# A written order of all tasks in place of a list rule, with another weight split, other first loads and two units' taps on TensorE

## The chip, the cores and the metric

One core of one Trainium2 chip runs the whole program. The metric is the device time in microseconds of one execution, the median over several. A profiled execution gives a trace: TensorE (PE, and PEld for its weight loads), VectorE (DVE), ScalarE (ACT), GpSimd (POOL) and the DMA queue of SyncE (SP).

## The reference, cut to what matters

The program is a local attention with a few global rows, followed by a gated layer over all heads. There are 8 batches and 8 heads; each head has 512 local rows and 32 global rows of width 64. A global row attends to all 544 keys; a local row to the 32 global keys and to the local keys within 32 positions.

```python
s_g = scale * np.matmul(q_g, k_all.transpose(0, 1, 3, 2))
out_g = np.matmul(sm(s_g), v_all)
...
s_ll = np.where(np.abs(pos[:, None] - pos[None, :]) <= 32, s_ll, -1000000000.0)
s_l = np.concatenate([s_lg, s_ll], axis=-1)
out_l = np.matmul(sm(s_l), np.concatenate([v_g, v_l], axis=2))
x = np.concatenate([out_g, out_l], axis=2)          # then heads side by side: (8, 544, 512)
...
for k in range(5):
    gate_pre += conv_w[k] * xp[:, k:k + S, :]       # causal, along the sequence
gate = 1.0 / (1.0 + np.exp(-gate_pre))
return (gate * (x @ w_val) @ w_out).astype(np.float32)
```

The inputs are float32, the three parameters of the gated layer float64.

## The kernel before, in words

**Units.** A unit is two heads of one batch, 128 channels: 32 units, four to a batch. Every piece of work is a task with a name, and the number in a name is the unit, or the batch for the global rows.

- `iq`, `iv` load a unit's queries and keys (a `qk` tile, 624 KB) and its values (a `v` tile, 975 KB); `fq`, `fv` mark the buffers free. There are four buffers of each.
- `s` (L419): 64 small fp32 matmuls, scores of 16 blocks of 32 rows against 128 keys, for both heads, into PSUM tiles sx and sy.
- `mx` u.h (L431), VectorE: adds the mask and takes the row minimum of the negated scores, four fused operations a head. `exp` (L438), ScalarE. `t` (L444): four transposes on TensorE. `tc` (L447): ScalarE copies them to SBUF.
- `av` (L455): 64 matmuls with the values. `norm` (L462, L463, L465), VectorE, divides by the sums. `xt` (L474): four transposes back. `xc` (L478): a ScalarE copy.
- `halo` (L483, L485) puts the last global rows ahead of the unit. `xh` (L503, ScalarE) rounds to the fast matmul format fp32r, `xl` (L506, VectorE) is the rest. So products are made of three matmuls: high times high, high times low, low times high.
- The gate is five taps along the sequence: `tap` (L497) and `conv` u.0 to u.3 (L510), all on VectorE. In the first NPC = 3 units they are fp32 matmuls with diagonal matrices instead: `dg` (L524, ScalarE makes the diagonals), `pc` u.0 to u.4 (L535), copied out by ScalarE (L540). The first NHF = 1 unit does not wait for the global rows and is mended by `fix` (L492).
- Global rows of a batch: `gs` (L344), `gmax` (L351 to L353), `gexp` (L360, L361), `gt` (L367 to L370), `gtc` (L376 to L378), `gav` (L387), `gnorm` (L393 to L395), `gx` (L399), `gxc` (L403).

**Gated layer.** `sig` (L543) is the sigmoid. `g1.b.e.t` (L559) multiplies by w_val, three matmuls for each input tile t and output tile e; `gv` (L567, VectorE) times the gate, `gh` (L570, ScalarE) and `gl` (L573, VectorE) split it, `g2.b.r.e` (L581) multiplies by w_out, `ob` (L586, ScalarE) copies out, `st` stores. The global rows of all batches go through it last, as batch g: `gxh`, `gxl` (L624, L627), `gconv` (L630, L632: one scaling and four taps each), `sigg`, then g1.g and g2.g.

**Weights.** The eight 128-row tiles of w_val and w_out come as float64 bits in pairs of int32. Tasks `w`k.s0 to s5 (L245 to L252) on VectorE rebuild a float32 value and a low remainder, ScalarE rounds the value to fp32r (`w`k.high, L297), and VectorE subtracts the rounded from the value (`less`, L301) and adds the remainder (`plus`, L304) to make the low part.

**Order.** The kernel is written task by task into strict in-order queues, one for each engine. `Plan.order` (L140 to L207) makes the order by a list rule: from planned durations, delays and buffer rings it computes when each ready task could begin, and takes the earliest, ties by the priorities PR. Nothing of it runs on the chip.

```python
                    if best is None or (at, t.prio) < best[0]:
                        best = ((at, t.prio), t)
```

**Start.** `first` lists the loads that are issued before the plan. GpSimd zeroes a tile zf, VectorE casts it to zr, and `keep_clock` (L641) issues matmuls of zeros: WARM = 4 at the start, and more in planned gaps over KEEP = 1500 ns until the first task that takes an `mm` PSUM bank.

Of the kernel before, what the change touches and what calls it, by code (L numbers as in the profile page):

```python
# [19 lines left out]
KW = 5  # L20
# [24 lines left out]
def pos_chunk(p):  # L45
# [3 lines left out]
PR = {'w': (2.1108, 2.3658, 2.2497, 1.6373, 1.8399, 2.1059, 1.8007, 2.1913),  # L49
      'whigh': 2.271,  # L50
      'gs': 4.588,
      'gmax': 2.96,
      's': 1.721,
      'mx': 0.684,
      'exp': 2.812,
      'norm': 1.347,
      'xl': 5.608,
      'tap': 3.042,
      'conv': 3.339,
      'pc': 5.493,  # L60
      'gv': -3.126,
      'gl': 0.929,
      'wi': -1.844,
      'cw': -4.483,
      'dg': 3.265,
      'sig': 1.801,
      'ob': 0.619,
      'gh': -3.407,
      'tc': 0.686,
      'xc': -1.569,  # L70
      'xh': 1.612,
      't': 1.915,
      'av': 3.833,
      'xt': 3.243,
      'g': 6.355,
      'gexp': 5.157,
      'gt': 2.783,
      'gtc': 1.05,
      'gav': 0.635,
      'gnorm': 1.312,  # L80
      'gx': -0.882,
      'gxc': 3.072,
      'fix': 4.315}
E1 = D + 1
NX = 10
NHF = 1
NQ = 4
WO = 2
NPC = 3
WARM = 4  # L90
# [15 lines left out]
class Task:  # L106
    __slots__ = ("name", "eng", "cost", "deps", "take", "give", "prio", "emit", "end", "start", "lock")

    def __init__(self, name, eng, cost, deps, take, give, prio, emit, lock):
        self.name, self.eng, self.cost, self.deps = name, eng, cost, deps  # L110
        self.take, self.give, self.prio, self.emit, self.lock = take, give, prio, emit, lock
        self.start = self.end = None


class Plan:
# [13 lines left out]
    def add(self, name, eng, cost, emit, deps=(), take=(), give=(), prio=5.0, lock=False):  # L129
        assert name not in self.tasks, name  # L130
        self.tasks[name] = Task(name, eng, cost, tuple(deps), tuple(take), tuple(give), prio, emit, lock)
# [8 lines left out]
    def order(self):  # L140
        users, missing, todo = {}, {}, {}
        done = dict(self.ready)
        for t in self.tasks.values():
            todo.setdefault(t.eng, [])
            names = {d for d in t.deps if d not in done}
            missing[t.name] = len(names)
            for d in names:
                users.setdefault(d, []).append(t)
            if not names:
                todo[t.eng].append(t)  # L150
        free = dict.fromkeys(todo, 0.0)
        held = dict.fromkeys(LOCKED, 0.0)
        mode, table = 2, 1
        line, base = [], {}

        def since(t):
            at = base.get(t.name)
            if at is None:
                at = base[t.name] = max([0.0] + [done[d] + self.lag(d, t) for d in t.deps])
            more = {}  # L160
            for name, _ in t.take:
                n, taken, freed = self.rings[name]
                k = len(taken) + more.get(name, 0) - n
                more[name] = more.get(name, 0) + 1
                if k >= 0:
                    if k >= len(taken) or taken[k] not in freed:
                        return None
                    at = max(at, freed[taken[k]])
            return at

        while len(line) < len(self.tasks):
            best = None
            for eng, ts in todo.items():
                for t in ts:
                    at = since(t)
                    if at is None:
                        continue
                    if t.lock:
                        at = max(at, held[LOCKED[eng == "DVE"]])
                    at = max(at, free[eng])  # L180
                    if best is None or (at, t.prio) < best[0]:
                        best = ((at, t.prio), t)
            if best is None:
                raise RuntimeError("nothing can begin: " + ", ".join(t.name for ts in todo.values() for t in ts))
            (at, _), t = best
            for name, key in t.take:
                self.rings[name][1].append(key)
# [10 lines left out]
            for name, key in t.give:  # L198
                assert key in self.rings[name][1], (t.name, name, key)
                self.rings[name][2][key] = t.end + LAG[t.eng]  # L200
            todo[t.eng].remove(t)
            for user in users.get(t.name, ()):
                missing[user.name] -= 1
                if not missing[user.name]:
                    todo[user.eng].append(user)
            line.append(t)
        return line  # L207
# [3 lines left out]
def attention_moe(ctx, tc, qk, vw, maskd, w_val, convT, w_out, out):  # L211
# [21 lines left out]
    xgT = cp.tile([P, NDT, B, KW - 1 + SG], F32, name="xgT")  # L233
    zf = sb.tile([P, SL], F32, tag="gv", name="zf")
# [3 lines left out]
    def f64_parts(raw, a, e, b):  # L238
# [5 lines left out]
        af = a.bitcast(F32)  # L244
        return (lambda: V.tensor_scalar(out=a, in0=hi, scalar1=0x7FFFFFFF, scalar2=None, op0=ALU.bitwise_and),  # L245
# [9 lines left out]
    def taps():  # L255
        raw = craw.rearrange("p (n two) -> p n two", two=2)
        a = sb.tile([P, NDT * KW], I32, tag="mx", name="cva", bufs=3)
        for step in f64_parts(raw, a, raw[..., 1], raw[..., 0].bitcast(F32)):
            step()
# [604 lines left out]
```

## Time and profile before

| | |
|---|---|
| median of three runs | 380.77 us (380.75 to 383.97) |
| profiled execution, its own time | 384.15 us |
| its span, first to last instruction | 382.3 us |
| instructions | 14802 |
| busy: PE, PEld | 363.6 us (95%), 281.9 us (74%) |
| busy: DVE, ACT, POOL | 312.0 us (82%), 263.7 us (69%), 2.2 us (1%) |
| mean granted TensorE clock | 0.993 |
| DMA | 66.74 MB, mean 175 GB/s |

In the rows of the profile, `PE po L581` is an engine, the tile that it writes and the line of the kernel; `x48` is a count of instructions; `<-ACT pm L438 3.0` says what ended an idle time, and for how many us. Matmuls are pipelined, so their durations overlap; what one costs TensorE is the distance to the next one's start. The same holds, by a smaller overlap, for VectorE and ScalarE. A wait on "issue" is time in which the engine waited for nothing that the profile shows.

### The profile page before, as it was taken

The numbers are of one execution on the slowest core, as the hardware profiler recorded it, in microseconds if no ns is written. First come the engines' busy times: TensorE is split into PE (matmuls) and PEld (weight loads), VectorE is DVE, ScalarE is ACT, GpSimd is POOL, SyncE is SP. The second block draws the span as 40 slices with busy tenths as digits, with TensorE's granted clock in tenths as the row PEclk, the third lists the DMA queues.
The fourth block names the chain that finished last, engine by engine and source line by source line (L and its number), as shares of the span: only waits on it lengthen the run. The fifth ranks groups of instructions, "written<-read, shape, count | busy, mean of one in ns | idle before, by whom it ended". The sixth has DMA issues, their size and how long they took to land.

```text
span 382.3 us, 14802 instructions
## 1 busy us (share of the span) xinstructions
PE 363.6 (95%) x6342; PEld 281.9 (74%) x6342; DVE 312.0 (82%) x1089; ACT 263.7 (69%) x624; POOL 2.2 (1%) x8
## 2 busy tenths in 40 slices
PE   6797999999999999999899979999999999999994
PEld 4455567777777788877777768777877888888893
DVE  4997999999968997689878987699699999996230
ACT  2986379966899578966795669659996776413221
POOL 2000000000000000000000000000000000000000
PEclk9998999999999999999999999999999999999998
DMA  8996873846521973556382646564663011020112
GB/s 274 406 405 236 295 259 115 280 179 230 187 69 38 394 269 107 223 189 224 117 310 77 235 141 182 231 186 155 256 210 106 4 57 58 0 83 29 55 57 56
DMA packets 17250, 66.74 MB, mean 175 GB/s; under 512 B 1952, under 2 KB 4000, under 8 KB 17184
## 3 DMA queue, kind: packets, MB, share of 16 engines
q1 hardware_dynamic: 17184, 65.79, 48.1%
q8 instruction: 50, 0.82, 0.9%
q14 instruction: 16, 0.13, 0.1%
HBM read 56.87 MB, written 8.91 MB: 172 GB/s over the span
## 4 chain that ended last, share of the span: by engine, by line
PE 62%; DVE 22%; ACT 10%; DMA 2%; issue 2%; SPq 0%; ACTq 0%
PE po L581 21%; PE pv L559 14%; PE ax L455 6%; PE pt L444 5%; ACT pm L438 5%; DVE gate L510 4%; PE sx L419 3%; PE ax L474 3%; DVE pm L431 2%; DVE gl L573 2%; PE ag L387 2%; DVE xs L465 2%; PE sy L419 2%; PE pvg L559 1%; PE pog L581 1%
## 5 line engine op out<-in xcount | busy, mean ns | idle before, releaser
L438 ACT ACTIVATE pm<-pm,mx 128x128 f32<-128x128 f32 x256 | 80.8, 393 | 17.9 <-DVE mx L431 17.8
L510 DVE SCALAR_TENSOR_TENSOR gate<-xc,cw,gate 128x512 f32<-128x512 f32 x116 | 84.5, 747 | 0.5
L581 PE MATMUL po<-woh,gh 128*128 128x512 f32 x128 | 54.4, 425 | 0.0
L559 PE MATMUL pv<-xh,wvh 128*128 128x512 f32 x128 | 54.0, 422 | 0.0
L559 PE MATMUL pv<-xl,wvh 128*128 128x512 f32 x128 | 50.6, 396 | 0.0
L581 PE MATMUL po<-woh,gl 128*128 128x512 f32 x128 | 50.4, 394 | 0.1
L559 PE MATMUL pv<-xh,wvl 128*128 128x512 f32 x128 | 50.5, 394 | 0.0
L581 PE MATMUL po<-wol,gh 128*128 128x512 f32 x128 | 50.1, 392 | 0.0
L444 PE MATMUL pt<-ident,pm 128*128 128x128 f32 x256 | 41.4, 284 | 4.0 <-ACT pm L438 3.8
L447 ACT COPY pts<-pt 128x512 f32<-128x512 f32 x64 | 36.8, 584 | 9.5 <-PE pt L444 9.3
L444 PEld LDWEIGHTS pt<-ident,pm 128*128 128x128 f32 x256 | 30.6, 142 | 14.3 <-ACT pm L438 5.8
L419 PE MATMUL sx<-qk 64*32 64x128 f32 x1024 | 38.7, 278 | 0.0
L419 PE MATMUL sy<-qk 64*32 64x128 f32 x1024 | 37.3, 278 | 0.1
L455 PEld LDWEIGHTS ax<-v,pts 128*32 128x32 f32 x2048 | 30.9, 111 | 7.6 <-issue 3.6
L419 PEld LDWEIGHTS sx<-qk 64*32 64x32 f32 x1024 | 29.3, 107 | 9.8 <-issue 4.6
L455 PE MATMUL ax<-v,pts 128*32 128x65 f32 x2048 | 36.2, 223 | 0.3 <-ACT xc L478 0.3
L586 ACT COPY ob<-po 128x512 f32<-128x512 f32 x32 | 18.8, 588 | 21.9 <-PE po L581 21.7
L570 ACT CAST gh<-gv 128x512 fp32r<-128x512 f32 x32 | 19.7, 617 | 17.8 <-DVE gv L567 17.8
L567 DVE TENSOR_TENSOR gv<-pv,gate 128x512 f32<-128x512 f32 x32 | 22.0, 688 | 11.1 <-PE pv L559 9.4
L431 DVE CUSTOM_DVE_ANT_0 pm<-sx,mask 128x128 f32<-128x128 f32 x128 | 29.4, 286 | 1.7 <-PE sx L419 1.6
L573 DVE TENSOR_TENSOR gl<-gv,gh 128x512 fp32r<-128x512 f32 x32 | 22.0, 689 | 10.5 <-ACT gh L570 10.4
L431 DVE CUSTOM_DVE_ANT_0 pm<-sy,mask 128x128 f32<-128x128 f32 x128 | 29.4, 287 | 0.0
(109 smaller groups left out, 658.4 us busy)
## 6 DMA issues: line engine op xcount, KB each, us to landing
v<-in_vw_dram SPq DMA_DIRECT2D x32, 975.0 KB, 7.7
qk<-in_qk_dram SPq DMA_DIRECT2D x32, 624.0 KB, 5.0
out_dram<-ob SPq DMA_DIRECT2D x32, 256.0 KB, 2.3
wraw<-in_w_val_dram SPq DMA_DIRECT2D x4, 512.0 KB, 12.3
wraw<-in_w_out_dram SPq DMA_DIRECT2D x4, 512.0 KB, 8.0
out_dram<-obg SPq DMA_DIRECT2D x8, 64.0 KB, 1.7
mask<-in_mask_dram SPq DMA_DIRECT2D x1, 256.0 KB, 4.2
craw<-in_convT_dram SPq DMA_DIRECT2D x1, 20.0 KB, 3.9
```

The source lines that it names most:

```text
L419: T.matmul((sx, sy)[h][32 * j:32 * j + 32, i, :], qkt[rows, 32 * m:32 * m + 32], qkt[rows, k0:k0 + P], start=True, stop=True)
L431: V.tensor_tensor_reduce(out=pm[:, h, i, :], in0=s[:, i, :], in1=mask[:, i, :], op0=ALU.add, op1=ALU.min, scale=-SCALE, scalar=3.0e38, acc ...
L438: A.activation(out=pm[:, h, i, :], in_=pm[:, h, i, :], func=AF.Exp, bias=mx[:, c:c + 1], scale=-1.0)
L444: T.transpose(pt[:, i, :], pm[:, h, i, :], ident)
L447: A.copy(st[u]["pts"][:, h], st[u]["pt", h])
L455: T.matmul(ax[32 * j:32 * j + 32, h, E1 * i:E1 * i + E1], pts[:, h, i, 32 * j:32 * j + 32], vt[:, block_win(4 * i + j), h, :], start=True, ...
L510: V.scalar_tensor_tensor(out=acc, in0=xc[:, k:k + SL], scalar=cw[:, u % NDT, k:k + 1], in1=acc, op0=ALU.mult, op1=ALU.add)
L559: T.matmul(box["pv", e], w[:, e, t * P:t * P + P], x, start=(t == 0 and q == 0), stop=(t == NDT - 1 and q == 2))
L567: V.tensor_tensor(out=box["gv", e], in0=box["pv", e], in1=gates[x0 + e], op=ALU.mult)
L570: A.copy(box["gh"][:, e, :], box["gv", e])
L573: V.tensor_tensor(out=box["gl"][:, e, :], in0=box["gv", e], in1=box["gh"][:, e, :].bitcast(F32), op=ALU.subtract)
L581: T.matmul(box["po", r], g[:, e, rs], w[:, e, :], start=(e == 0 and q == 0), stop=(e == NDT - 1 and q == 2))
```

## The change

It does five things.

1. The list rule and its priorities go. `ORDER` is a text of 1494 task names; each engine gets its tasks in that order. `Plan.order` still computes planned times, for the filler matmuls alone.
2. The weights are split by bits: step s2 keeps 12 bits fewer, so that the value in `a` is already the high part. The low part is made of the bits left over by four more VectorE steps (s4 to s7 in place of s4, s5, less and plus). ScalarE's rounding copy `high` stays. (`PW` names no tile, so the branch with GpSimd is not taken; `NXP` = 0 likewise.)
3. First loads: q3 moves from behind v0 to ahead of it.
4. Start: zf is zeroed on VectorE, ScalarE runs one exponential on it, and warm-up is two fp32 matmuls of zf and one of zr (WARM 4 to 1). Of xgT only the halo columns are zeroed. Fillers for gaps become more numerous (0.55 for 0.4 of the gap).
5. NPC goes from 3 to 2, NHF from 1 to 2: units 0 and 1 have their taps on TensorE and are mended by `fix`. NTA = 4: `tap` of units 2 and 3 goes to ScalarE.

```diff
-PR = {'w': (2.1108, 2.3658, 2.2497, 1.6373, 1.8399, 2.1059, 1.8007, 2.1913),
...
+ORDER = """
+cw s0 mx0.0 exp0.0 mx0.1 w0.s0 exp0.1 first s1 mx1.0 exp1.0 w0.s1 t0.0 w0.s2 tc0.0 t1.0 tc1.0 t0.1 mx1.1 tc0.1 gs0
+w0.s3 w0.s4 w0.s5 w0.s6 gmax0.0 dg0 exp1.1 av0 gexp0.0 iq4 t1.1 gmax0.1 w1.s0 iq5 gexp0.1 s2 norm0 lq4 tc1.1 xt0 w1.s1
+w0.s7 w1.s2 w0.high mx2.0 mx2.1 xc0 exp2.0 halo0 gt0.0 w2.s0 w1.s3 av1 w2.s1 norm1 s3 w1.s4 pc0.0 w2.s2 dg1 w1.s5
...
+g1.2.3.3 sig11 conv15.3 gv.2.2 sig12 gl.2.1 gv.2.3 mx19.0 xt17 mx19.1 gt4.1 gh.2.2 lq20 g2.2.0.0 xl16 gl.2.2 xc17
+g2.2.0.1 iq23 av18 lq23 gtc4.1 gh.2.3 gav4.1 s20 g2.2.0.2 tap16 sig13 gnorm4.1 gx4 gl.2.3 mx20.0 exp19.1 g2.2.0.3 gxc4
...
+st.6.3 g1.7.3.0 gxl2 gv.7.2 gxh3 st.6.2 g1.7.3.1 g1.7.3.2 g1.7.3.3 gh.7.2 g2.7.0.0 g2.7.0.1 gl.7.2 g2.7.0.2 gv.7.3
+gh.7.3 gl.7.3 g2.7.0.3 gconv3 gxl0 g2.7.1.0 g2.7.1.1 g2.7.1.2 ob.7.0 gconv0 g2.7.1.3 g2.7.2.0 gconv1 g2.7.2.1 gconv2
+g2.7.2.2 st.7.0 ob.7.1 st.7.1 g2.7.2.3 g2.7.3.0 g2.7.3.1 g2.7.3.2 ob.7.2 g2.7.3.3 g1.g.0.0 g1.g.0.1 g1.g.0.2 ob.7.3
+gxl3 sigg g1.g.0.3 st.7.3 gv.g.0 st.7.2 g1.g.1.0 gh.g.0 g1.g.1.1 g1.g.1.2 g1.g.1.3 g1.g.2.0 g1.g.2.1 gl.g.0 g1.g.2.2
...
+"""
+PW = "x"
+NXP = 0
+FIRST = "q0 m0 q1 w0 q2 q3 v0 w1 v1 w2 v2 w3 v3"
+NTA = 4
-NHF = 1
+NHF = 2
-NPC = 3
-WARM = 4
+NPC = 2
+WARM = 1
...
-                    if best is None or (at, t.prio) < best[0]:
-                        best = ((at, t.prio), t)
...
+        for name in ORDER.split():
+            put(self.tasks[name])
...
+        kept = 0x3FFFFFF8 if low is None else 0x3FFFF000
...
+        power = lambda: V.tensor_scalar(out=hi, in0=a, scalar1=-0x00800000, scalar2=None, op0=ALU.bitwise_and)
+        scaled = lambda x, out: V.scalar_tensor_tensor(out=out, in0=x, scalar=2.0 ** -52, in1=hf, op0=ALU.mult,
+                                                       op1=ALU.mult)
...
+        return first + (lambda: V.tensor_scalar(out=hi, in0=hi, scalar1=0x1FF, scalar2=None, op0=ALU.bitwise_and),
+                        lambda: V.scalar_tensor_tensor(out=lf, in0=hi, scalar=2.0 ** 32, in1=lo.bitcast(U32),
+                                                       op0=ALU.mult, op1=ALU.add),
+                        power, lambda: scaled(lf, low))
...
-        plan.add(f"w{k}.less", "DVE", 570, less, [f"w{k}.high", f"w{k}.s5"], prio=prio - 0.01, lock=True)
-        plan.add(f"w{k}", "DVE", 570, plus, [f"w{k}.less"], give=back, prio=prio - 0.02, lock=True)
...
+        if u < NTA:
+            A.activation(out=g, in_=x, func=AF.Copy, scale=w)
+        else:
+            V.tensor_scalar(out=g, in0=x, scalar1=w, scalar2=None, op0=ALU.mult)
...
-        G.memset(zf, 0.0)
-        V.tensor_copy(zr, zf)
-        G.memset(xgT, 0.0)
+        G.memset(xgT[:, :, :, :KW - 1], 0.0)
+        A.activation(out=table, in_=zf[:, :1], func=AF.Exp)
+        keep_clock(2, zf)
         keep_clock(WARM)
...
-                    keep_clock(int((gap - 300) * 0.4 / 235))
+                    keep_clock(int((gap - 400) * 0.55 / 235))
```

378 lines of the change are left out of this document (198 added, 180 removed).

## The prediction, as it went on record

> **What bounds the kernel now.** I read the stage windows first, then the end of the chain of waits, then the groups of TensorE and VectorE on both sides of 182.5 us.
>
> The rows give length, then busy us (and instructions) of TensorE, its weight load, VectorE, ScalarE and GpSimd, the granted TensorE clock, DMA share and GB/s.
>
> ```profile
> 0.00:40.00 40.00, 31.25 (x641) 20.20 (x645) 31.36 (x128) 28.16 (x77) 2.16 (x8) 0.96 0.85 317
> 40.00:100.00 60.00, 59.33 (x1205) 42.99 (x1204) 59.13 (x214) 42.44 (x107) 0.00 (x0) 1.00 0.65 229
> 100.00:182.50 82.50, 82.50 (x1577) 65.25 (x1566) 68.66 (x258) 66.64 (x152) 0.00 (x0) 1.00 0.53 187
> 182.50:322.60 140.10, 135.96 (x2684) 108.12 (x2683) 121.53 (x435) 109.34 (x258) 0.00 (x0) 1.00 0.45 156
> 322.60:382.30 59.70, 54.54 (x262) 45.37 (x260) 31.29 (x62) 17.13 (x32) 0.00 (x0) 0.98 0.14 49
> ```
>
> The reader is to see three stages. Until 40 us nothing is full: loads at 317 GB/s, TensorE and VectorE waiting for each other. From 40 to 100 us TensorE (59.33 of 60) and VectorE (59.13) are both full. After 100 us TensorE alone is full and VectorE has slack (13.8 us idle of 82.5). ScalarE never binds for long. The end is pure TensorE:
>
> ```profile
> 355.10 10.91 PE po L581 x48
> 366.01 5.69 PE pvg L559 x48
> 371.70 5.46 PE pog L581 x24
> ```
>
> That is 0.227 us for a product matmul of 512 columns, 0.119 us for one of 256, and a last matmul that is over at 377.16, 5.1 us before the span ends. So the time is TensorE's work, plus what TensorE waits in the head and in a few later places, plus 5.1 us.
>
> **The change, part by part.** The forecast is made at one cut: the moment when the new list lets g2.2.0.3 start (third batch, second product, the one that waits for gl.2.3). Up to there VectorE's list is the longest demand; behind it TensorE's is.
>
> *Remaining work behind the cut.* These TensorE groups ran in the old kernel from 182.5 us to its last matmul:
>
> ```profile
> L581 PE MATMUL po<-woh,gh 128*128 128x512 f32 x83 | 34.8, 419 | 0.0
> L559 PE MATMUL pv<-xh,wvh 128*128 128x512 f32 x80 | 33.1, 413 | 0.0
> ...
> L455 PE MATMUL ax<-v,pts 128*32 128x65 f32 x960 | 16.7, 221 | 0.0
> L444 PE MATMUL pt<-ident,pm 128*128 128x128 f32 x112 | 16.7, 276 | 3.0 <-ACT pm L438 3.0
> L419 PE MATMUL sx<-qk 64*32 64x128 f32 x416 | 15.0, 273 | 0.0
> ...
> L474 PE MATMUL ax<-ident,xs 128*128 128x128 f32 x64 | 10.1, 278 | 1.0 <-issue 1.0
> ```
>
> In tasks: 83 second products of the batches (and 8 of the global stage), 80 first products, 15 av, 28 t, 13 s (416 of sx and as many of sy), 16 xt. Counted in the written list from g2.2.0.3 on: 93 and 8 second products, 80 first ones, 13 av, 26 t, 11 s, 14 xt. Ten second products more (30 matmuls of 0.227 = 6.8 us) against two av, two t, two s, two xt and three small tasks fewer. With the busy times of the rows (16.7/15 an av, 16.7/28 a t, 15.0/13 an s, 10.1/16 an xt) the four pairs are 7.0 us. So the work behind the cut equals that of the old kernel behind 182.5 us, which took 377.16 - 182.5 = 194.7 us, 4.0 of it waits (3.0 for an exponential, 1.0 called issue). (The busy times hold an overlap with the next task, which the three small tasks make up.)
>
> *When the cut comes, by VectorE.* Its work before 182.5 us in the old kernel:
>
> ```profile
> L510 DVE SCALAR_TENSOR_TENSOR gate<-xc,cw,gate 128x512 f32<-128x512 f32 x47 | 34.2, 747 | 0.2
> ...
> L431 DVE DVE_READ_ACCUMULATOR2_ANT mx<- 128x1 f32 x148 | 12.5, 84 | 0.0
> L465 DVE TENSOR_TENSOR xs<-ax,mx 128x512 f32<-128x512 f32 x17 | 11.8, 692 | 0.6
> L506 DVE TENSOR_TENSOR xl<-xc,xh 128x512 fp32r<-128x512 f32 x15 | 10.3, 688 | 0.6 <-ACT xh L503 0.5
> ...
> L395 DVE TENSOR_SCALAR xg<-ag,gd 128x64 f32<-128x64 f32 x9 | 2.6, 284 | 0.3
> ...
> L492 DVE SCALAR_TENSOR_TENSOR gate<-xgT,cw,gate 128x4 f32<-128x4 f32 (+3 forms) x4 | 0.9, 220 | 0.1
> ```
>
> An instruction's share of the engine is its distance to the next start, some 0.09 us under its duration:
>
> ```profile
> 20.43 0.71 DVE L249 SCALAR_TENSOR_TENSOR wa<-wraw,wa 128x512 int32<-128x512 int32 x1
> 21.04 0.70 DVE L506 TENSOR_TENSOR xl<-xc,xh 128x512 fp32r<-128x512 f32 x1
> 21.64 0.43 DVE L245 TENSOR_SCALAR wa<-wraw 128x512 int32<-128x512 int32 x1
> 21.98 0.45 DVE L251 TENSOR_SCALAR wraw<-wa 128x512 int32<-128x512 int32 x1
> ...
> 24.79 0.30 DVE L431 CUSTOM_DVE_ANT_0 pm<-sx,mask 128x128 f32<-128x128 f32 x1
> ...
> 25.00 0.30 DVE L431 CUSTOM_DVE_ANT_0 pm<-sx,mask 128x128 f32<-128x128 f32 x1
> ```
>
> So an operation with two tensors holds VectorE 0.60, one with a scalar 0.34, a tap (747 ns) 0.66, a masked maximum (four with their reads, each 0.21) 0.85.
>
> The written list has ahead of gl.2.3: 56 taps on VectorE against 47 (+5.9, four of them because unit 2 loses its TensorE taps), 40 half maxima against 148/4 = 37 (+2.5), 18 norms against 17 (+1.0), 17 xl against 15 (+1.2), one more norm of the global rows and one more set of four halo fixes (together +1.5). All eight weight tiles lie ahead in both. A tile was four short and four long operations (s0, s1, s2, s4; s3, s5, less, plus): 3.76 us; now five short and three long (less and plus give way to an AND and a multiply-add inside the raw words, then power and scale): 3.50, so -2.1 for eight. The new operations have no row; the nearest, L245 and L251 with a stride on one side and L249 with one on an input, give 0.34 and 0.60, and I take these; strided on both sides they could cost 0.60 instead of 0.34, at most +2.1 in all, and not less than nothing. Sum: +10.0.
>
> VectorE's old busy time up to 182.5 us is 31.36 + 59.13 + 68.66 = 159.2, of which 1.2 come before its real start:
>
> ```profile
> 1.80 1.24 DVE L788 CAST zr<-zf 128x512 fp32r<-128x512 f32 x1 [1.80 <-POOL zf L787]
> 5.61 0.18 DVE L245 TENSOR_SCALAR cva<-craw 128x20 int32<-128x20 int32 x1 [2.57 <-DMA craw<-in_convT_dram]
> ```
>
> The new kernel needs 158.0 + 10.0 = 168.0 us from 5.6 on. Idle to add, by VectorE's waits of the first 100 us:
>
> ```profile
> DVE mx L462 <- PE ax L455: 1.6, 1, 1.6
> DVE wa L245 <- DMA wraw<-in_w_val_dram: 0.8, 1, 0.8
> DVE wa L301 <- ACT wvh L297: 0.5, 1, 0.5
> DVE gd L393 <- PE ag L387: 0.4, 1, 0.4
> ```
>
> The third is gone, since the low part no longer waits for ScalarE's rounded copy; 2.8 stay. From 40 to 100 us VectorE lost 0.87 in 60; over the 138 us to the cut 2.0. Cut at 5.6 + 168.0 + 4.8 = 178.4 us.
>
> *The same by TensorE.* Five fp32 taps of unit 2 go. Sixteen instructions, two to a tap, show their price:
>
> ```profile
> 43.42 7.03 PE L535 MATMUL pc<-xc,diag 128*128 128x512 f32 x16
> ```
>
> 0.43 each, so 5 x 2 x 0.43 = 4.3 us. TensorE at the old pace would be at the cut at 182.5 - 4.3 = 178.2. The two engines agree within 0.2 us: the first half gains 4.1 us, and neither has room to spare.
>
> *Head.* ScalarE's first exponentials start late:
>
> ```profile
> 7.15 1.28 ACT L524 ACT_TABLE_LOAD   x1 [7.15 <-DVE cw L260]
> ...
> 9.92 2.44 ACT L438 ACTIVATE pm<-pm,mx 128x128 f32<-128x128 f32 x8
> ```
>
> The table load moves ahead of the data and the first diagonals behind the exponentials: up to 2.8 us for ScalarE, of which I count nothing, because VectorE's demand hides it; without that cover it would be a gain. v0 behind q3 costs av0 a qk tile's transfer and gives it to gs0, which the list puts ahead of av0: nothing. The two zero-filled fp32 warm-up matmuls (four instructions, 0.43 at full clock, 0.86 at half, so 1.7 to 3.4 us) run before the first scores have data, and cw is ahead of the first maximum anyway: nothing, at worst 0.3.
>
> *Behind the cut.* A written order can place an exponential earlier: the 3.0 us go (they could all return). The 1.0 called issue stays. Changes between kinds of TensorE task are 299 in the old timeline and 301 in the list: nothing. SP's queue is reordered too; I followed each load from the task that frees its buffer to its first user. Most have over 8 us; v14, v15, v23 and v24 have 5 to 7: nothing, at worst 1 us each. ScalarE gets two taps of 0.5 us and loses unit 2's diagonals and its copy: hidden.
>
> At the tail the list puts all four global taps behind gl.7.3, and gxl3 behind them:
>
> ```profile
> 335.07 0.35 DVE L630 TENSOR_SCALAR gateg<-xgT,cw 128x256 f32<-128x256 f32 x1
> 335.45 2.05 DVE L632 SCALAR_TENSOR_TENSOR gateg<-xgT,cw,gateg 128x256 f32<-128x256 f32 x4
> ```
>
> After the last g1.7 VectorE needs about 2.2 us for gv and gl with ScalarE's copy between, 4 x 2.43 for these taps, and two splits of 0.34: 12.6 us. TensorE has 10.91 us of second products and three parts of g1.g (9 x 0.119 = 1.1) before g1.g.0.3 wants gxl3: it waits 0.6 us, 0 to 1.
>
> Sum: 178.4 + 194.7 - 3.0 + 0.6 + 5.1 = 375.8 us against a span of 382.3, so -6.5. The profiled execution's own time was 384.15 us, 1.85 more than its span and 3.4 above the median of the runs, 380.77 (380.75 to 383.97); I take the difference off the median: **374.3 us**.
>
> **Rivals.**
>
> *TensorE was the only limit.* VectorE idles 2.0 instead of 4.8, no wait returns, the issue wait and the tail wait go: -2.8 - 1.6, 369.9 us. For it: the loads of the head leave ScalarE's 2.8 us on the table. Against it: the two sums above agree, so each engine's waits become the other's.
>
> *The gain turns into new waits.* The order is fixed for planned durations; where an instruction is late, all behind it on its engine wait. VectorE idles 8 us (+3.2), the 3.0 us for exponentials come back: 380.5 us. For it: VectorE's idle was 4.2 us in the head and up to 100 us (3.3 of the rows above and 0.87) even under a rule that was free to choose. Against: that rule planned blind too.
>
> *The clock.* Once in the old head, after 1.05 us of TensorE work in 3.0, the granted clock halved for a stretch (first fence), though the longest gap was under 2 us (second):
>
> ```profile
> 28.20:31.20 3.00, 1.05 (x51) 0.73 (x41) 2.65 (x18) 2.14 (x7) 0.00 (x0) 1.00 1.01 412
> 32.13:35.55 3.42, 3.18 (x50) 2.45 (x52) 2.38 (x6) 3.06 (x7) 0.00 (x0) 0.50 0.53 173
> ```
>
> ```profile
> 30.68 0.55 PE L387 MATMUL ag<-v,pgt 96*32 96x65 f32 x23 [1.95 <-issue]
> ```
>
> Such a stretch costs up to 1.7 us. Filler matmuls stop at the first pc0.0, fourteenth on TensorE's list, while VectorE's demand still grows 6.5 us faster than TensorE's work between s4 and g1.0.0.3, by the prices above. Two more stretches: +3.4, 377.7 us. The Trainium skill (TensorE: Matmul & The Clock Gate, "Why this matters for your kernels") says that gaps up to about 3 us between bursts are safe; by that rule these stretches cost nothing and the forecast stands. The trace is stricter, since 1.95 us was enough.
>
> *Slower.* From 100 us to the cut VectorE idled 13.8 us, harmlessly, since it was ahead. If the strict list makes it idle as much while it is the limit, waiting for scores or products that are listed late, its idle at the cut is 4.8 + 13.8 = 18.6 and the cut 13.8 us later: 388.1 us. It decides from 15.1 us of idle on (4.8 plus the 10.3 us between 374.3 and 1% above the old median). For it: the list has no second choice. Against: 40 to 100 us show 0.87 idle in 60 when VectorE has a backlog.
>
> *It does not do what it says.* The rounded high part is still ScalarE's copy; if the new bit operations cost the upper bound, +2.1, 376.4: inside the range.
>
> **How the numbers follow.** Forecast 0.57 (370.5 to 376.9), TensorE alone 0.10, new waits 0.15, clock 0.10, slower 0.08. A measurement here tells about 1% from no change, 377.0 to 384.6 being the same. Faster 0.57 + 0.10 = 0.67, same 0.15 + 0.10 = 0.25, slower 0.08. The range runs from just above the first rival, 370.0, to 381.0, half a microsecond above the new waits: left out are half the first rival and the slower case and a little of the waits.
>
> **What would show it.** In the new profile: 20 pc matmuls instead of 30; VectorE over 97% busy from 40 us to the cut, and the cut (the 36th second product's start) near 178 us; behind it TensorE without a wait over 1.5 us; g1.g waiting half a microsecond for xgl. I am wrong if VectorE idles over 8 us after 40 us with TensorE idle in the same places, or if the cut is in time and the second half has new waits, of loads above all.

## The result, and the profile after

The new kernel takes 400.18 us (median; 396.43 to 403.6) against 381.31 us for the old one on the same chip: ratio 1.042, 95% interval 1.037 to 1.048. The forecast was 374.3 us: the change is slower where I expected it faster, and the miss is 26 us. The profiled execution took 399.97 us with a span of 397.3.

The stage windows of the new kernel, in the same cuts and columns as in the prediction:

```profile
0.00:40.00 40.00, 29.86 (x647) 18.40 (x648) 30.68 (x142) 25.26 (x71) 0.85 (x7) 0.96 0.81 303
40.00:100.00 60.00, 53.73 (x1013) 39.00 (x1012) 54.36 (x186) 40.24 (x95) 0.00 (x0) 1.00 0.57 211
100.00:182.50 82.50, 77.67 (x1768) 61.21 (x1774) 74.31 (x284) 66.05 (x166) 0.00 (x0) 1.00 0.59 202
182.50:322.60 140.10, 130.56 (x2467) 105.42 (x2468) 109.74 (x394) 104.22 (x237) 0.00 (x0) 0.98 0.44 154
322.60:397.30 74.70, 69.85 (x453) 57.56 (x451) 42.87 (x94) 29.46 (x57) 0.00 (x0) 0.98 0.14 50
```

From 40 to 100 us, where the old kernel had TensorE busy for 59.33 of 60 us and VectorE for 59.13, TensorE now has 6.3 us of holes and VectorE 5.6, in the same stage. TensorE's busy time over the whole span hardly changed (363.6 us before, 361.7 after); what grew is its idle time. Summed over all its waits above 0.1 us from 5 us on, it is 10.4 us before and 29.4 after. The new kernel's table of waits of TensorE (total, times, longest):

```profile
PE sx L466 <- ACT pg L408: 7.0, 4, 3.1
PE sx L466 <- issue: 6.9, 5, 3.5
PE ax L502 <- DMA v<-in_vw_dram: 4.5, 2, 2.2
PE sy L466 <- issue: 2.0, 1, 2.0
...
PE ax L502 <- issue: 1.7, 1, 1.7
```

Three kinds. "issue" is a wait for nothing that the profile shows (scores, line 466, and av, line 502, stop in the middle of a task). "ACT pg" are scores that wait until the exponentials of a batch's global rows (`gexp`, L408) have freed sx and sy. "DMA v" are av0 and av24, whose values are late. In the old kernel the first kind was there, in part under another name; the other two were not.

**Where "issue" comes from.** The page's list of DMA queues has one that no line of the kernel uses:

```profile
q8 instruction: 49, 0.80, 0.8%
```

These are 49 packets of 16,384 bytes. TensorE's stream has 6334 matmuls, as many weight loads and 78 semaphore instructions, 12,746 in all, which is 63 bytes an instruction: a packet holds about 256 of them, and nearly the whole stream comes this way. The packets follow TensorE's progress: 40 of the 49 begin to move within 4 us after TensorE has begun the packet before. And the "issue" stops of both kernels that are longer than half a microsecond stand at one place in a packet: counted along TensorE's stream, after 193 instructions and then after each further 256. Two of them in the new kernel's timeline:

```profile
31.48 0.27 PE L466 MATMUL sy<-qk 64*32 64x128 f32 x1
35.22 0.30 PE L466 MATMUL sx<-qk 64*32 64x128 f32 x2 [3.47 <-issue]
...
187.59 1.11 PE L502 MATMUL ax<-v,pts 128*32 128x65 f32 x64
188.52 0.75 PE L434 MATMUL ag<-v,pgt 96*32 96x65 f32 x40
...
189.87 0.27 PE L466 MATMUL sx<-qk 64*32 64x128 f32 x1
191.20 0.29 PE L466 MATMUL sx<-qk 64*32 64x128 f32 x1 [1.06 <-issue]
```

In the second, av18 (128 instructions), a gav (80) and s20 (128) stand back to back: TensorE runs through 256 instructions in some 2 us, and the next packet is not there. The times of the transfers on that queue, which the trace holds, settle it: each of the new kernel's eight stops ends 1.2 to 1.6 us after a packet has landed (the one that ends at 35.22 us had its packet moved from 32.67 to 33.68), and so do the stops over 0.3 us at packets' edges in every other trace of this study but one (1.0 us).

The same count finds the old kernel's stops: at 30.7, 183.7, 224.4 and 262.2 us (idle for 1.95, 1.00, 2.28 and 0.71 us). The last two are the prediction's "3.0 for an exponential", since the profile names ScalarE's pm there; but the four exponentials that the transposes at 224.36 read were over at 221.30, and the packet landed at 222.91. In the old kernel, the row of TensorE, then that of ScalarE:

```profile
224.36 0.60 PE L444 MATMUL pt<-ident,pm 128*128 128x128 f32 x4 [2.28 <-ACT pm L438]
```

```profile
220.02 1.28 ACT L438 ACTIVATE pm<-pm,mx 128x128 f32<-128x128 f32 x4
```

So the 3.0 us, the "1.0 called issue" and the 1.95 us of the clock rival, three things in the prediction, were one and the same.

The written order has TensorE's tasks of many short matmuls (`s`, `av`, `gs`, `gav`) directly behind one another 34 times, the old list 22 times. (That count alone does not decide: order_edges_counted below has 33 such pairs and one stop. What should count is whether a whole packet of 256 runs through too soon.) The kernel's planner sees none of this: it puts the end of TensorE's work at 369.7 us in the old kernel and at 365.2 in the new one.

### The profile page after: what moved, and what is told of

Same layout as the page of the kernel before. It is cut to its first block, busy times and chain, and to the rows that moved or that the text cites. A ratio compares the mean times of both kernels' runs of the same rounds, so it can differ in the third digit from the quotient of the medians.

```text
span 397.3 us, 14784 instructions
## 1 busy us (share of the span) xinstructions
PE 361.7 (91%) x6334; PEld 281.6 (71%) x6334; DVE 312.0 (79%) x1097; ACT 265.2 (67%) x623; POOL 0.8 (0%) x7
## 4 chain that ended last, share of the span: by engine, by line
PE 68%; DVE 13%; DMA 10%; issue 4%; ACT 4%; SPq 0%; ACTq 0%; DVEq 0%
PE pv L609 19%; PE po L631 16%; PE ax L502 7%; PE sx L466 6%; PE pt L491 6%; DMA wraw<-in_w_val_dram 3%; PE ax L521 3%; DMA out_dram<-ob 3%; PE sy L466 2%; DVE gate L560 2%; PE ag L434 2%; DVE gateg L681 2%; PE pc L585 2%; DMA v<-in_vw_dram 2%; PE pog L631 1%
## 5 line engine op out<-in xcount | busy, mean ns | idle before, releaser
L560 DVE SCALAR_TENSOR_TENSOR gate<-xc,cw,gate 128x512 f32<-128x512 f32 x120 | 88.1, 747 | 0.9
L609 PE MATMUL pv<-xh,wvh 128*128 128x512 f32 x128 | 54.8, 428 | 0.0
L466 PE MATMUL sx<-qk 64*32 64x128 f32 x1024 | 40.3, 279 | 14.1 <-ACT pg L408 7.0
L466 PEld LDWEIGHTS sx<-qk 64*32 64x32 f32 x1024 | 29.5, 108 | 23.1 <-issue 10.3
L466 PE MATMUL sy<-qk 64*32 64x128 f32 x1024 | 38.7, 279 | 2.0 <-issue 2.0
L491 PE MATMUL pt<-ident,pm 128*128 128x128 f32 x256 | 38.6, 277 | 1.0 <-DVE mx L509 0.5
L478 DVE CUSTOM_DVE_ANT_0 pm<-sx,mask 128x128 f32<-128x128 f32 x128 | 29.4, 286 | 12.6 <-PE sx L466 12.5
L478 DVE CUSTOM_DVE_ANT_0 pm<-sy,mask 128x128 f32<-128x128 f32 x128 | 29.4, 286 | 0.0
L466 PEld LDWEIGHTS sy<-qk 64*32 64x32 f32 x1024 | 27.1, 107 | 2.7 <-issue 2.2
```

The costliest lines, as they stand in the source:

```text
L466: T.matmul((sx, sy)[h][32 * j:32 * j + 32, i, :], qkt[rows, 32 * m:32 * m + 32], qkt[rows, k0:k0 + P], start=True, stop=True)
L478: V.tensor_tensor_reduce(out=pm[:, h, i, :], in0=s[:, i, :], in1=mask[:, i, :], op0=ALU.add, op1=ALU.min, scale=-SCALE, scalar=3.0e38, acc ...
L491: T.transpose(pt[:, i, :], pm[:, h, i, :], ident)
L560: V.scalar_tensor_tensor(out=acc, in0=xc[:, k:k + SL], scalar=cw[:, u % NDT, k:k + 1], in1=acc, op0=ALU.mult, op1=ALU.add)
L609: T.matmul(box["pv", e], w[:, e, t * P:t * P + P], x, start=(t == 0 and q == 0), stop=(t == NDT - 1 and q == 2))
```

## The experiments

Three theories are set against each other. FETCH: TensorE's instructions come in packets, and short matmuls use one up before the next is there. LOADS: what is lost are the waits for loads, and for what stands behind loads in SyncE's queue. ORDER: a written list loses whatever is late, because it has no second choice.

The table holds all runs that are compared with the old kernel. "Idle" is TensorE's idle time as above, in the profiled execution; "edges" the stops at packets' edges, from one matmul's start to the next, where that is over 0.35 us and TensorE was idle; "half clock" the stretches at half the granted clock before the last matmul. Each ratio is to runs of the old kernel beside it on the same chip; its medians there were 381.31, 382.28, 382.56, 383.14 and 382.60 us.

| kernel | us | ratio to old (95%) | last matmul ends | idle | edges | half clock |
|---|---|---|---|---|---|---|
| old | 381.31 | | 377.1 | 10.4 | 7.4 | 1 |
| new | 400.18 | 1.042 (1.037 to 1.048) | 392.6 | 29.4 | 13.3 | 3 |
| after_no_reload | 383.46 | 1.003 (0.999 to 1.006) | 375.7 | 15.6 | 5.9 | 1 |
| before_no_reload | 377.89 | 0.988 (0.984 to 0.991) | 371.4 | 6.2 | 0.9 | 1 |
| after_store_scalar | 405.85 | 1.062 (1.056 to 1.068) | 397.9 | 29.4 | 11.8 | 5 |
| old_order_old_start | 380.51 | 0.996 (0.992 to 0.999) | 372.7 | 8.1 | 4.8 | 0 |
| old_order_new_start | 383.85 | 1.004 (1.000 to 1.007) | | | | |
| order_without_packets | 391.28 | 1.024 (1.018 to 1.031) | 378.7 | 21.0 | 8.7 | 1 |
| order_with_packets | 380.49 | 0.995 (0.991 to 0.998) | 373.3 | 13.3 | 6.9 | 1 |
| order_edges_counted | 377.05 | 0.984 (0.980 to 0.989) | 368.5 | 10.1 | 0.9 | 0 |
| order_edges_old_start | 375.64 | 0.981 (0.976 to 0.987) | 365.7 | 6.4 | 1.6 | 0 |
| order_no_spread | 375.94 | 0.982 (0.977 to 0.986) | 369.2 | 8.8 | 5.6 | 1 |
| order_old_durations | 383.91 | 1.003 (1.000 to 1.007) | 375.8 | 15.3 | 3.6 | 1 |
| order_free_transfers | 381.86 | 0.998 (0.996 to 1.001) | 374.8 | 14.6 | 2.3 | 1 |
| order_packets_only | 390.41 | 1.020 (1.014 to 1.027) | 384.4 | 21.3 | 3.4 | 4 |

(The profiled execution of order_without_packets was its fastest, 387.41 us; of old_order_new_start only the time is used.)

### The packets by themselves

The whole computation is left out. TensorE runs the second attention product of a unit (`av`, 64 short matmuls, 128 instructions) again and again, alone and with product matmuls of 512 columns between, without and with loads.

```diff
+        bursts(24, 0)
+        product(20)
+        bursts(12, 4)
+        product(20)
+        bursts(12, 8)
...
+        for u in range(24):
+            nc.sync.dma_start(many[u % 12], qk[u])
+        product(20)
+        bursts(24, 0)
```

> Measures the instruction packets by themselves and leaves out the whole computation: 24 units' second attention products (64 short matmuls and 64 weight loads each, 128 instructions in about 1.05 us) back to back; then 12 of them with 4 product matmuls between, then with 8; then the 24 and the 12 with 8 again while 24 tiles of 1.6 us are being loaded. FETCH: back to back, each 256 instructions take 3.0 to 3.7 us instead of 2.1, with a stop at each packet's edge; with 4 products between (256 instructions less the products' in about 3.6 us) hardly a stop; with 8 none; while tiles load, 4 to 7 us for 256 instructions back to back and stops even with 8 products between. The rival (the gaps called issue come from something else that TensorE waits for, a bank or a weight register): no stop at packets' edges, 2.1 us for 256 instructions.

TensorE's timeline in the quiet part, then with 24 tiles under way:

```profile
47.57 2.02 PE L73 MATMUL ax<-vt,pts 128*32 128x65 f32 x128 [1.16 <-issue]
51.02 2.02 PE L73 MATMUL ax<-vt,pts 128*32 128x65 f32 x128 [1.44 <-issue]
54.48 2.02 PE L73 MATMUL ax<-vt,pts 128*32 128x65 f32 x128 [1.44 <-issue]
...
174.60 3.69 PE L73 MATMUL ax<-vt,pts 128*32 128x65 f32 x128 [3.73 <-issue]
180.52 3.56 PE L73 MATMUL ax<-vt,pts 128*32 128x65 f32 x128 [2.23 <-issue]
186.72 3.27 PE L73 MATMUL ax<-vt,pts 128*32 128x65 f32 x128 [2.63 <-issue]
```

A run of exactly 128 matmuls (256 instructions) and a stop, with a period of 3.45 us (51.02 - 47.57, 54.48 - 51.02) in nine of eleven packets. So here a packet begins 3.45 us after the one before it, however short the work in it; 2.02 us of short matmuls leave 1.44 us of idle. It is no lower bound for every kernel: in the new one the stop at 272.5 us ends 2.9 us after the packet before began, and at 316.6 us a packet follows after 1.9 us without a stop; that one began to move 1.3 us before TensorE had begun the packet before. With four products between two bursts no stop is over 0.35 us. While loads move 417 GB/s, the period is 5.8 to 6.2 us, and two stops of 0.6 and 0.8 us come even with eight products between. The 128 matmuls take 3.3 to 3.7 us there instead of 2.02: the granted clock is 0.69 in the mean, as the windows of the quiet and of the loaded part show (last columns: clock, DMA share, GB/s):

```profile
44.33:82.38 38.05, 22.26 (x1425) 20.58 (x1414) 0.00 (x0) 0.00 (x0) 1.00 0.02 5
168.79:199.11 30.32, 15.30 (x657) 14.36 (x646) 0.00 (x0) 0.00 (x0) 0.69 1.02 417
```

The rival (a bank, a weight register) falls: every stop stands at a packet's edge and ends 1.3 to 1.6 us after a packet has landed.

### The loads

```diff
+        if u >= NQ:
+            loads.setdefault(u, [None, None])[0] = loads[u % NQ][0]
+            return
         t = sb.tile([P, QK], F32, tag="qk", name=f"qk{u}", bufs=NQ)
```

and the same for the v tiles; six lines more, so that L466 becomes L472. First in the new kernel, then in the old one.

> The new kernel in which units 4 to 31 load nothing and reuse the tiles of units 0 to 3, so every load after the head is left out (and with it the data of those units). Three theories of the 15 us by which TensorE's last matmul came later (392.2 against 376.75 us). FETCH: TensorE's own instructions arrive in packets of 256, one packet ahead, and a run of short matmuls can use up a packet before the next is there; loads on the same DMA engines make a packet later still. Then the stops at the edges of packets (13.3 us of gaps, 8 of them) shrink but those where 256 instructions run in under about 3.5 us stay at the edge: 3 to 5 us left. LOADS: what is lost is the wait for v and qk tiles and what stands behind loads in SyncE's queue (v0, v24, the stores that hold up ScalarE's copy and the exponentials behind it): about 8 us go, the stops at the packets' edges stay as they are. ORDER: the list loses by having no second choice, whatever is late: the time stays above 394 us. FETCH with LOADS together says 380 to 387 us, LOADS alone 390 to 393, ORDER 394 to 400.

> The old kernel with the same loads left out, as the control. Its stops at the edges of packets were 6.7 us in 4 places, its waits for loads after the head nothing. FETCH: 1 to 4 us faster, 377 to 380 us. LOADS: within 1 us of 381. ORDER: within 1 us of 381. If both kernels gain the same, the loads do not explain the difference between them.

The new kernel gains 16.7 us without its loads, the old one 3.4 to 4.4 (377.89 against 381.31 and 382.28). So some 13 of the 19 us between the two need the loads, and 5.6 stay without them. The new kernel's waits without loads:

```profile
PE sx L472 <- ACT pg L414: 4.4, 4, 1.6
...
PE sx L472 <- issue: 1.6, 2, 0.8
```

The stops at edges fall from 13.3 to 5.9 us (FETCH had 3 to 5) but stay where 256 instructions run in about 3 us, as FETCH said. LOADS alone (390 to 393) and ORDER (394 to 400) both miss; FETCH with LOADS (380 to 387) holds.

### Stores past SyncE's queue

One wait looked like a queue's fault. At 245 us TensorE waits 3.1 us for s25. ScalarE's rows there, then the rows of SyncE's queue:

```profile
244.20 0.62 ACT L553 CAST xh<-xc 128x512 fp32r<-128x512 f32 x1
247.03 0.59 ACT L636 COPY ob<-po 128x512 f32<-128x512 f32 x1 [2.21 <-DMA out_dram<-ob]
247.51 0.40 ACT L407 ACTIVATE pg<-gs,gm 128x160 f32<-128x160 f32 x1
```

```profile
230.42 0.38 SPq L792 DMA_DIRECT2D out_dram<-ob  x1
240.91 0.33 SPq L366 DMA_DIRECT2D qk<-in_qk_dram  x1
241.33 7.12 SPq L792 DMA_DIRECT2D out_dram<-ob  x3
```

The qk load of unit 28 waits until 240.91 for its buffer, three stores wait behind it, a copy on ScalarE waits for one of these stores to leave its buffer, and the exponential that frees sx for s25 stands behind the copy. So:

```diff
-                   lambda r, o, b=b: nc.sync.dma_start(out[b, SG + r * P:SG + r * P + P, :], o))
+                   lambda r, o, b=b: nc.scalar.dma_start(out[b, SG + r * P:SG + r * P + P, :], o))
```

> The new kernel with the stores issued from ScalarE's queue, behind its own copy, instead of from SyncE's, where they stand behind loads that wait for a buffer. LOADS (its part on SyncE's queue): the 5.8 us that ScalarE waits for stores to leave their buffer, with the 3 us that TensorE waits for the exponential behind it near 245 us, go: 395 to 397 us against 400. FETCH and ORDER: the waits of ScalarE go but no more than 1 to 3 us of the time, 397 to 400.

It is 5.7 us slower than the new kernel (405.85 against 400.18), outside every expectation, with five half-clock stretches instead of three. ScalarE's wait for stores rises from 5.8 to 13.4 us in all, and TensorE still waits 2.8 us for the exponential before s25: a store issued from ScalarE's strict queue no longer waits behind a load, but it waits behind everything that the list puts between the copy and the store on ScalarE, and the next copy waits for it. Moving one kind of work to another queue in an order written for the first queue only made another wait here. Why it is slower in all, and not equal, I did not settle.

### The order with and without the packets

To test the order, I made others from it: a model replays a written list with the kernel's own planner (costs, delays, rings), with or without what the planner lacks, and single tasks are moved in the list as long as that brings the end of TensorE's work forward. Nothing but the list changes in the kernel. TensorE's tasks of the list around s20, with the others left out, in the new kernel and in order_edges_counted:

```diff
-gt4.1 g2.2.0.0 g2.2.0.1 av18 gav4.1 s20 g2.2.0.2 gx4 g2.2.0.3 g2.2.1.0 t19.1
+av18 gav4.1 g2.2.0.3 g2.2.1.0 gx4 s20 t19.0 g2.2.1.1 g2.2.1.2 g2.2.1.3 g2.2.2.0
```

> The new kernel with another written order and nothing else changed. It was searched from the new one with three things in the planner that it lacks: a packet of 256 TensorE instructions is there 3.45 us after the one before it began (measured in the packets' own run) and up to 2.75 us later while loads are under way; transfers land in the order in which they are issued; some spread in the durations. The kernel's own planner gives it the same planned end as the new order, 365.2 against 365.2 us. FETCH with LOADS (the order's packets and transfers are the loss): no stop at a packet's edge over 0.5 us, TensorE's last matmul near 371, 374 to 381 us in all. ORDER (any written order loses its lateness on the way): 393 to 400 us.

> The same search with the packets left out of the planner (transfers in the order of issue and the spread of durations kept). Planned end 364.0 us, 1.2 us ahead of its twin. FETCH: 10 to 12 us of stops at packets' edges by the model, so 8 to 12 us slower than its twin, 384 to 392 us. LOADS alone: as fast as the twin within 2 us. ORDER: 393 to 400 like the new kernel.

The twins differ by 10.8 us in the time, though the kernel's planner gives the one without packets an end 1.2 us earlier: in the times FETCH with LOADS holds, and both its rivals miss. The stops fit less well. FETCH had none over 0.5 us with the packets and 10 to 12 us without them; the traces have 6.9 and 8.7. Of the 7.7 us between the two idle times (13.3 and 21.0) only 1.8 stand at edges, so this pair alone does not show that the packets make the difference. The six stops in the order with packets are all from 144 us on, where the count of instructions had drifted. With the semaphore instructions counted:

> As the order with packets, which kept six stops at packets' edges (6.9 us) from 144 us on: there TensorE's queue holds some 80 semaphore instructions that its planner had not counted, so that its edges drifted from the true ones. Now they are counted (0.6% more instructions). Planned end 365.0 us. FETCH: at most 2 us of stops left, 4 to 6 us faster than the order with packets: 374.5 to 377 us. If the rest is other lateness (ORDER): within 2 us of 380.5.

377.05 us: 3.4 us faster, just short of what FETCH said, with one stop of 0.9 us left. It is the new kernel with nothing but its list replaced, and 23 us faster, so the loss is the list's and not the split's or the start's. Against the order without packets the last matmul ends 10.2 us earlier, and 7.8 us of stops are gone. TensorE's waits, first in the order without packets, then in this one:

```profile
PE sx L466 <- ACT pg L408: 4.6, 2, 2.6
PE sx L466 <- issue: 3.3, 2, 2.4
```

```profile
PE sx L466 <- ACT pg L408: 4.0, 3, 1.6
...
PE sy L466 <- issue: 0.7, 1, 0.7
```

### What else the planner lacks

Was it also that a written list has no room for lateness? One search more without any spread in its durations, and three that each leave one or both of the other two corrections out: durations as measured, and transfers that land in the order in which they are issued. (In the kernel's planner a transfer is a task of its own, placed by the list; in the new list 16 of 60 are placed behind one that is issued after them, in the old one none.)

> The same search with packets, their edges counted and transfers in order of issue, on the new start, but for one set of durations only: nothing in it allows for late transfers or uneven tasks. Planned end 364.8 us. FETCH with LOADS: within 2 us of its twin with the spread, 375 to 378. ORDER (an order without room for lateness loses it on the way, packets or not): 5 us or more behind the twin, 381 to 390.

> Searched like the order without spread (packets counted, transfers in the order of issue), but with the new kernel's own planned durations in place of the measured ones (scores 1.0 where the trace has 1.09, a weight's steps 0.32 and 0.54 where it has 0.34 and 0.60, the exponentials of the global rows 0.75 where the next scores follow them later). Planned end 364.4 us. If the new kernel's 16 us of waits away from the packets' edges came from its durations: 8 us or more behind the order without spread (375.9), 384 or more. By the planner with the measured durations it loses 3.1 us: 377 to 381.

> Searched with packets counted and measured durations, but transfers placed by the list, as in the new kernel's planner, and not in the order in which they are issued. Its planner believes 365.4 us; with its own transfers in the order of issue 370.0. If the transfers make the difference (LOADS): 4 to 8 us behind the order without spread, 380 to 384. If not: within 2 us of it.

> Searched with the packets counted and everything else as the new kernel's planner has it (its durations, transfers placed by the list). That planner believes 364.1 us; with its own transfers in the order of issue 381.3, and 384.3 with the measured durations. If this is how the new kernel loses what the packets leave (LOADS): 388 to 396 us with hardly a stop at a packet's edge, most of it in waits for v and qk tiles. If the packets were all: 375 to 380.

Without spread: 375.94 us, no worse than its twin. ORDER, the theory that was my "slower" rival, falls as a cause: this list is as strict as the new one and 24 us faster. So is the old list written out (380.51, below), and the old rule too had fixed every queue before the run. The planner's durations cost 8.0 us (383.91 against 375.94; my model had 3), its free transfers 5.9, both together 14.5: the two add up. Leaving the packets out costs 14.2 (391.28 against 377.05), or 9.8 on top of the other two (the new kernel against order_packets_only's 390.41). Each of these is one list against one other. How far two lists from the same planner differ by chance was not measured, and stops alone do not set the time: the order without spread has 5.6 us of them, its twin 0.9, and is 1.1 us faster. What I had expected of order_packets_only, waits mostly for v and qk tiles, is not what its rows show; the largest is a product behind a copy that waits for a store (10.9 us on ScalarE):

```profile
PE pv L609 <- ACT ob L636: 4.2, 1, 4.2
...
PE ax L502 <- DMA v<-in_vw_dram: 2.2, 1, 2.2
```

```profile
ACT ob L636 <- DMA out_dram<-ob: 10.9, 2, 7.0
```

So here a transfer out of its planned place hit through the stores that stand behind it; that this is the rule is not shown.

### The split and the start, one by one

The old list written out, with the new weight split in place of the old one (for each weight, the tasks less and plus give way to s6 and s7 in the list); then with the new first loads and warm-up as well. The shorter zeroing of xgT is in both.

```diff
-FIRST = "q0 m0 q1 w0 q2 v0 q3 w1 v1 w2 v2 w3 v3"
-WARM = 4
+FIRST = "q0 m0 q1 w0 q2 q3 v0 w1 v1 w2 v2 w3 v3"
+WARM = 1
```

> The list that the old kernel's rule makes, written out; of the change only the split of the weights by bits is in (three units' taps on TensorE, first loads and warm-up as in the old kernel). If the loss is the order's (FETCH, LOADS or ORDER alike): within 1.5 us of the old kernel, 380 to 382. If the new bit operations cost what I bounded at most (2.1 us) or hold up GpSimd or ScalarE: 383 or more.

> As the one before it, with the new first loads and the new warm-up as well. If these cost what the head of the new kernel shows (v0 late, a lower clock at 36 us): 2 to 4 us slower than it. If the head of the new kernel is its order's: within 1.5 us of it.

The split alone: 380.51 us, ratio 0.996 (0.992 to 0.999), half a per cent faster, as said for the case that the loss is the order's. The new start on top: 383.85, 3.3 us slower, and the intervals don't touch. To see whether that was the start or an old list that did not fit it:

> The same search and planner, on the old first loads and the old warm-up (the new split, two units' taps on TensorE as in the new kernel). Planned end 365.5 us. If the new start costs what the two old orders showed (3.3 us, 383.85 against 380.51), this one is 2 to 4 us faster than its twin on the new start: 372 to 374.5. If that cost was only that the old list did not fit the new start: within 1.5 us of the twin.

1.4 us faster than its twin on the new start, with intervals that overlap: within what was said for a misfit, and too little to call the new start a loss. It has the lowest median of the study, 0.3 us below order_no_spread, and is 1.9% faster than the old kernel (1.3 to 2.4%). Its windows, cut at 40, 100, the start of g2.2.0.3 and the end of the last matmul:

```profile
0.00:40.00 40.00, 33.70 (x707) 21.22 (x707) 32.68 (x137) 27.13 (x73) 1.42 (x8) 1.00 0.87 324
40.00:100.00 60.00, 57.01 (x1156) 42.65 (x1148) 57.70 (x212) 44.48 (x110) 0.00 (x0) 1.00 0.59 221
100.00:173.20 73.20, 73.17 (x1647) 58.83 (x1645) 71.01 (x275) 65.11 (x156) 0.00 (x0) 1.00 0.60 213
173.20:365.70 192.50, 192.50 (x2840) 156.97 (x2838) 149.31 (x477) 132.33 (x287) 0.00 (x0) 1.00 0.36 127
```

The cut came at 173.2 us, and behind it TensorE is busy without a hole for 192.5 us.

## Why the prediction was wrong, point by point

The prediction's cut, the start of g2.2.0.3, came at 192.4 us instead of 178.4. The new kernel's windows on both sides of it:

```profile
5.60:40.00 34.40, 25.70 (x643) 16.87 (x643) 29.77 (x140) 23.77 (x69) 0.00 (x0) 0.95 0.83 320
40.00:192.40 152.40, 140.24 (x3033) 107.41 (x3032) 137.40 (x506) 115.17 (x278) 0.00 (x0) 1.00 0.57 200
192.40:392.60 200.20, 191.55 (x2658) 155.78 (x2656) 143.87 (x452) 124.22 (x273) 0.00 (x0) 0.98 0.33 119
```

- **VectorE's work up to the cut: right.** 29.77 + 137.40 = 167.2 us against 168.0. The new bit operations cost what I took for them: the AND that is strided on both sides (L294) takes 427 ns, as one strided on a single side (L283, 426).
- **"Idle to add" on VectorE: wrong, and the largest term.** 4.8 us were added; measured are 192.4 - 5.6 - 167.2 = 19.6, 4.6 of them up to 40 us and 15.0 behind. I took the idle time of the old list (2.8 in the head, 2.0 later) for the new one. That was the claim that a list planned like the old one waits like the old one. VectorE was busy for 90% from 40 us to the cut, where over 97% was the sign of being right, and TensorE was idle for 12.2 us of the same stage: the first of the two signs of being wrong. What VectorE waited for, up to 200 us, was mostly TensorE:

```profile
DVE pm L478 <- PE sx L466: 6.2, 7, 1.8
DVE mx L509 <- PE ax L502: 4.0, 6, 1.6
...
DVE gd L440 <- PE ag L434: 3.0, 1, 3.0
```

- **"The 1.0 called issue stays", and "changes between kinds of TensorE task ... nothing": the step behind it.** I counted how often the kind of task changes (299 and 301) and took the order within TensorE for free. What costs is how many instructions stand together: a packet of 256 that was used up sooner had to wait for the next one, 3.45 us from packet to packet in the quiet part of fetch_alone, 5.8 to 6.2 with loads under way. Stops at edges are 13.3 us against 7.4. That they cost more than their own length, through the clock and VectorE's waits, is likely from the 14 us between the lists with and without packets, but not shown for this list.
- **Work behind the cut: 200.2 us instead of 192.3** (194.7 - 3.0 + 0.6), with 191.55 busy. The amount was right; the idle is 8.65 us instead of 1.6. "A written order can place an exponential earlier: the 3.0 us go" failed twice: the old 3.0 were two packets' edges (2.28 and 0.71 us), and new waits for the global rows' exponentials came, 7.0 us in all, 3.1 of them behind the cut.
- **Loads "nothing, at worst 1 us each": wrong** for v24, one of the four that I had named (2.24 us), and for v0 in the head, where I had costed q3's transfer at nothing (2.2 us). And the loads slow the packets, a coupling that I had no term for: without them the two kernels differ by 5.6 us instead of 19.
- **Tail: right.** g1.g waits 0.17 us for xgl (forecast 0.6, 0 to 1), and the span ends 4.7 us behind the last matmul (5.1).
- **Median against span.** I took 1.5 us off the span, since the old profiled execution stood 3.4 us over its median. The new one stands at its median, 2.9 us over its span: 4.4 us of the miss.

Sum: 14.0 (cut) + 7.9 (behind it) - 0.4 (tail) + 4.4 = 25.9 us.

Of the rivals, "slower" came nearest: it put VectorE's idle at 18.6 us and the time at 388.1, for 8 in 100. Its effect was right and its reason, that a strict list has no second choice, was not: order_no_spread is as strict. "The clock" was right in its count, three half-clock stretches of 3.4 us, but not in their cause: it expected gaps in the head where TensorE waits for VectorE, and the gaps were a packet's edge (at 35 us), the wait for s25's exponential and the late v24. The Trainium skill (TensorE: Matmul & The Clock Gate, "Why this matters for your kernels") has gaps up to about 3 us as safe; two of the three stretches go with stops of 3.47 and 3.13 us, which agrees, the third with one of 2.24, which does not.

What stays open: of the 19.0 us by which TensorE's idle time grew (10.4 to 29.4), 5.0 stand at packets' edges, 7.0 are waits for the global rows' exponentials, 4.5 for late values, and the rest is spread. I can name single pieces (the 3.47 us stop at 35 us, s25, v24, the clock), but how far the waits follow from earlier stops, and what each thing that the planner lacks took from this very list, is not shown. The taps of two units in place of three, and the two taps on ScalarE, were not tested by themselves.

## What to carry to other kernels

Count TensorE's instructions, not only its time: where many short matmuls stand together, 256 instructions (weight loads and semaphore instructions included) in less than some 3 us can stop it, and more so while large loads run; put long matmuls between bursts, and look for stops that recur every 256 instructions behind a wait called "issue". An order that is written out is as good as its planner's picture of the machine: planned ends of 364.0 to 365.5 us became 375.6 to 400.2 on the chip, depending on whether packets, transfers in order of issue and measured durations were in the plan. A plan's gain of 4.4 us says nothing as long as the plan misses the trace by more.

## What the runs showed of the hardware that I had not expected

- Instructions come as data: TensorE's 0.8 MB on a queue of their own, in packets of 16,384 bytes, one ahead. Back to back, the next one is there 3.45 us after the one before began when the DMA engines are quiet, 5.8 to 6.2 us at 417 GB/s; a stop ends 1.2 to 1.6 us after its packet has landed.
- The profile can put such a stop down to another engine: the old kernel's 2.28 us at 224.4 stood as a wait for ScalarE.
- A repeated stop of 2.2 to 3.7 us halved the clock for much of the time (0.69 on average), so a packet's stop can cost the work behind it too. A single stop of 2.24 us did so (at 258 us), one of 1.97 did not (at 214 us).
- The half-clock stretches lie on a grid of steps of 3.413 us: in the new kernel they start at 36.44, 248.06 and 258.30 us, 62 and 3 steps apart. What went before them is a step with little work and not one long gap: of 31 steps at half clock before the last matmul in all traces here, 28 came behind a step in which TensorE was busy for 4 to 52% (of the other three, two behind one at half clock, one in before_no_reload behind 87%). The stop at 258 us fell into one step, the one at 214 us across an edge at 213.93.
